# A planned instruction order for a recurrent attention kernel: weight loads with release times, one shared DMA server in the planner, and a priority for each tile and row

## The chip, the cores and the metric

The kernel runs on one core of a Trainium2 chip. Five instruction streams work side by side: TensorE (PE; its weight loads are shown apart as PEld), VectorE (DVE), ScalarE (ACT), GpSimd (POOL) and SyncE (SP), which here only issues DMAs. Each stream takes its instructions strictly in the order in which they were written, and waits at an instruction until what it needs is there. The metric is the device time of one execution in microseconds; lower is better. The kernel before takes 223.28 us (median of 3 executions, 223.24 to 225.57). The profiled execution shows a span of 219.2 us from the first to the last instruction; the span leaves out 4.1 us that the metric counts.

## The reference, cut to what matters

The inputs r, k, v, w, a and b are [batch 4, heads 8, time 768, 40] in 32-bit floats. A 40x40 state for each batch and head goes through the 768 steps:

```
y[t]  = r[t] @ state
Sa    = state @ a[t]
state = state * w[t] - outer(Sa, b[t]) + outer(v[t], k[t])
```

The heads of y are put side by side to x, [4, 768, 320], and a mixing layer follows:

```
theta = x @ w_theta                     # 320x320
y     = w_tok_r @ (x*cos(theta)) + w_tok_i @ (x*sin(theta))   # both 768x768, over time
u     = x + y
out   = u + relu(u @ w_ch)              # 320x320
```

The token matrices mix all 768 steps of a batch, so no output row of a batch can be finished before all of its x is known.

## The kernel before, in words

**Tiles.** Time is cut into chunks of 128 steps, six to a batch, so there are 24 tiles (batch x chunk), numbered 0 to 23. All eight heads of a tile are worked on together. For each tile there are six loads of 160 KB (w, k, b, a, r, v; `loads`, L398, issued by SP) into buffers that exist four times (`raw_w`, `raw_kb`, `raw_a`, `raw_rv`). The innermost run of a load is one head's 40 floats, 160 bytes.

**Work of a tile.** `prep`: ACT takes the logarithm of w (`ln`, L407), PE sums it over time (`cs`, L414 to L424), ACT takes the exponential (`exp`, L429), POOL scales k, b and a with it and casts r and v (`kb`, `ah`, `rv`, L436 to L445; for tiles 0 and 1 DVE and ACT do this), PE transposes the results (`tkb`, `ta`, `trv`, L380) and ACT copies the transposes out of PSUM. `scores`: 64-row matmuls (L468) and a masking by DVE (L473), four times a tile. `recurrence`: `x0`, `nu`, `gt`, `gd`, `nut`, which pass the state from one tile of a batch to the next. `readout`: y, and x from it (`y`, `ex`, `xt`). `theta` (`th`, L616): three 320-column matmuls by `wth`, copied to a buffer. Once a half batch has its thetas, ACT computes cosines and sines (`sines`), which needs another ACT table than `ln` and `exp`, and POOL multiplies them with x (`z`, L652).

**Rows of the mixer.** `mix_row`, six to a batch, 24 in all: 12 matmuls of 320 columns (L671) against the transposed token matrices, an add (`uadd`, DVE), a transpose (`ut`), the product by `wch` (`ch`, L616), the last step on DVE (`oo`, L691) and the store by SP (`st`, L695). Row j needs block j of both token matrices.

**Weights.** POOL issues all weight loads: `wth` and `wch` in two DMAs each (`mixer_weights`, L701 and L704), and for each of six blocks of 128 rows one DMA for either token matrix (`wtok_block`, L712) into staging buffers `wrow`, two for each matrix. PE transposes a block (`wt`, L720) and DVE copies it into place, which sets the staging buffer free for the block after the next.

**Who sets the order.** The kernel writes its own order. Every step above is an `Op` with an engine, a modelled cost, what it reads and writes, and a priority; `Plan.order` runs a simulation in which, whenever an engine is free, the ready operation with the least `priority + wait * (time it would idle)` is taken. The instructions are then emitted in the order of planned start. Nothing of the plan's times exists on the chip: there only the order on each engine is left, and the semaphores. In the kernel before, the priority is `PERIOD * tile + OFF[kind]` (and `ROWLAG`, `ROWSTEP` for rows), so all tiles follow one rhythm; SP's and POOL's DMAs have two servers with separate queues in the plan; PE changing between 64-row and 128-row matmuls costs 91 ns in it. The six loads of tiles 0, 1 and 2 and those of tile 3 are ready at once, and so are the loads of `wth`, `wch` and of the first two token blocks.

Of the kernel before, what the change touches and what calls it, by code (L numbers as in the profile page):

```python
# [17 lines left out]
LAT = {("PE", "ACT"): 36, ("PE", "DVE"): 38, ("ACT", "PE"): 52, ("DVE", "PE"): 52,  # L18
       ("POOL", "PE"): 53, ("ACT", "DVE"): 33, ("ACT", "POOL"): 77}
OVERLAP = {"ACT": 94, "DVE": 83, "POOL": 50}  # L20
FREE0 = {"PE": 800, "ACT": 2100, "DVE": 4400, "POOL": 3600, "SP": 740}
BANKS = 8
DOUBLE = 4


class Op:
    __slots__ = ("eng", "kind", "i", "fn", "cost", "tail", "reads", "writes", "prio",
                 "mode", "table", "new", "spare", "pre", "nsucc", "start", "end", "idx",
                 "npre", "succ", "work", "banks", "soft", "loose")


class Plan:
# [7 lines left out]
    def add(self, eng, kind, i, fn, cost, reads=(), writes=(), prio=0.0, mode=128,  # L40
            tail=0, table=None, new=None, spare=0, work=0, after=(), loose=False):
        o = Op()
        o.eng, o.kind, o.i, o.fn, o.cost, o.prio = eng, kind, i, fn, cost, prio
        o.mode, o.tail, o.table, o.new, o.spare, o.work = mode, tail, table, new, spare, work
        o.reads, o.writes, o.loose = reads, writes, loose
        o.idx = len(self.ops)
# [18 lines left out]
    def order(self, wait=47.7, tswitch=11847.0):  # L65
        ops = self.ops
        for o in ops:
            o.succ = []
            o.npre = len(o.pre)
            o.start = o.end = None  # L70
            o.banks = None
        users = {}
        for o in ops:
            for k in set(o.reads) | set(o.writes):
                if k[0] == "ps":
                    users.setdefault(k, set()).add(o)
# [7 lines left out]
        for o in ops:  # L84
            for p in o.pre:
                p.succ.append(o)
            for p in o.soft:
                p.succ.append(o)
        left = {k: len(v) for k, v in users.items()}
# [8 lines left out]
        dma = [0.0, 0.0]  # L98
# [9 lines left out]
        def make_ready(o):  # L108
            t = 0.0
# [21 lines left out]
        while len(out) < n:  # L131
            pick = None
            for e, lst in ready.items():
                if not lst:
                    continue
                te = free[e]
                cand = []
                lo = None
                for o in lst:
# [8 lines left out]
                    if e == "PE" and o.mode != mode:  # L148
                        t += 91
# [6 lines left out]
                for t, o, b in cand:  # L156
                    s = o.prio + wait * (t - lo)
                    if e == "ACT" and o.table is not None and o.table != table:
                        s += tswitch
# [21 lines left out]
            elif o.work:  # L181
                q = 0 if o.eng == "SP" else 1
                iss = 430 if o.eng == "SP" else 890
                free[o.eng] = t + iss
                s = max(dma[q], t + iss + 900)
                if q == 1 and dma[0] > s:
                    dma[0] += o.work
                    dma[1] = s + 2 * o.work
                else:
                    dma[q] = s + o.work  # L190
                o.end = dma[q] + 1000
# [26 lines left out]
def tail(n):  # L218
# [3 lines left out]
OFF = dict(load=-32.72, ln=-14.21, cs=-14.27, exp=-12.91, kb=-24.2, ah=-17.45, rv=-8.81,  # L222
           tkb=-12.03, ekb=-12.49, ta=-6.68, ea=-13.73, spsi=-4.74, mpsi=3.81, sphi=-3.67,
           mphi=-0.3, trv=-7.1, erv=-4.13, slv=-1.2, mlv=12.94, x0=-1.29, nx=-1.28,
           nu=-1.19, enu=-4.96, gt=3.22, egt=5.53, gd=-0.91, egd=-4.34, nut=0.71,
           enut=-1.87, slu=0.59, mlu=4.85, y=4.31, ex=0.1, xt=7.27, ext=6.43, th=11.06,
           eth=17.93, sin=5.35, z=1.67, row=13.39, uadd=1.12, ut=13.16, eut=16.3, ch=19.9,
           oo=11.33, st=19.28, wdma=-32.85, wt=-13.25, ewt=-5.52)
PERIOD = 7.54
ROWLAG = 7.44  # L230
ROWSTEP = 7.6
# [3 lines left out]
def kernel(  # L235
# [130 lines left out]
    def prio(kind, i):  # L366
        return 1000.0 * (PERIOD * i + OFF[kind])

    def add(eng, kind, i, fn, cost, reads=(), writes=(), pr=None, **kw):
        return plan.add(eng, kind, i, fn, cost, tuple(reads), tuple(writes),  # L370
                        prio(kind, i) if pr is None else pr, **kw)
# [16 lines left out]
    def evac(eng, kind, i, psk, dst, n, reads=(), writes=()):  # L388
        if eng == "ACT":
            add(eng, kind, i, lambda: copy_words(dst, ps(psk)[:, 0:n // 2]),  # L390
                190 + n / 2.4, [psk], writes)
# [409 lines left out]
```

## Time and profile before

| What | Value |
|---|---|
| Time (median of 3) | 223.28 us |
| Span of the profiled execution | 219.2 us |
| PE busy | 198.0 us, 90% |
| DVE busy | 167.2 us, 76% |
| ACT busy | 147.1 us, 67% |
| POOL busy | 119.2 us, 54% |
| Bytes moved by DMA | 30.81 MB, mean 141 GB/s |
| A load of one of the six inputs, issue to landing | 3.7 to 4.1 us (medians) |
| A load of a token block, issue to landing | 4.7 and 5.1 us (medians) |

Busy times of an engine count the time in which at least one of its instructions is under way. Matmuls overlap: one of 320 columns lasts some 300 ns in the trace, while the next starts 136 ns later. So a PE that is shown busy all the time may still be waiting between short bursts, and how densely it works is better read from the spacing of its starts. Besides the busy times, the profile gives the busy share in 40 slices of the span, the chain of work that ended last, waits by who waited for whom, and tables by stage.

### The profile page before, as it was taken

How to read it: one execution, taken by the hardware profiler on the slowest of the kernel's cores; microseconds unless marked ns; L12 is line 12 of the kernel's file. 1: busy time of each engine (PE TensorE's matmuls, PEld its weight loads, DVE VectorE, ACT ScalarE, POOL GpSimd, SP SyncE). 2: the span in 40 equal slices, each digit the busy share in tenths (PEclk: the TensorE clock that was granted, in tenths of full speed). 3: DMA queues.
4: the chain of work that ended last, by engine and by line, in shares of the span. 5: the costliest groups of instructions: out<-in, count | busy, mean ns of one | idle time of the engine just before them, and what ended most of it. 6: DMA issues, size and time to landing. Idle time of an engine off the chain costs nothing.

```text
span 219.2 us, 8154 instructions
## 1 busy us (share of the span) xinstructions
PE 198.0 (90%) x3368; PEld 155.4 (71%) x3368; DVE 167.2 (76%) x250; ACT 147.1 (67%) x319; POOL 119.2 (54%) x184
## 2 busy tenths in 40 slices
PE   1519999889987999999999999999999999999992
PEld 1418778667776788878778778877877788776671
DVE  7336899885898759898598878869888889975532
ACT  3316755886769984996689766987698759563110
POOL 5600536798737791794938644986187507514000
PEclk9999999999999999999999999999999999999999
DMA  6999999999999899999999999999980000100121
GB/s 113 199 185 191 154 168 174 176 178 152 174 187 170 152 172 185 153 155 189 191 187 155 178 189 183 167 184 190 178 182 33 3 33 30 34 33 30 64 88 60
DMA packets 155684, 30.81 MB, mean 141 GB/s; under 512 B 150400, under 2 KB 155648, under 8 KB 155648
## 3 DMA queue, kind: packets, MB, share of 16 engines
q1 hardware_dynamic: 153216, 27.54, 68.9%
q0 software_dynamic: 2432, 2.77, 8.0%
q8 instruction: 26, 0.43, 0.8%
q14 instruction: 10, 0.08, 0.1%
HBM read 29.13 MB, written 3.93 MB: 151 GB/s over the span
## 4 chain that ended last, share of the span: by engine, by line
PE 74%; DMA 7%; DVE 6%; POOL 3%; ACT 3%; issue 3%; SPq 2%; DVEq 0%; ACTq 0%; POOLq 0%
PE ps_s L671 18%; PE ps_s L380 15%; PE ps_d L468 11%; PE ps_s L616 9%; DMA raw_w<-in_w_dram 7%; PE ps_s L572 4%; PE ps_s L538 2%; PE ps_s L520 2%; SPq L398 2%; PE ps_s L602 2%; PE ps_s L508 2%; DVE lamu L473 2%; PE ps_s L600 2%; DVE psi L473 2%; PE ps_s L502 1%
## 5 line engine op out<-in xcount | busy, mean ns | idle before, releaser
L436 POOL TENSOR_TENSOR kb<-raw_kb,ex 128x320 bf16<-128x320 f32 x44 | 37.1, 863 | 49.7 <-ACT ex L429 49.1
L671 PE MATMUL ps_s<-zr,wtok_r 128*128 128x320 bf16 x144 | 40.8, 300 | 0.0
L671 PE MATMUL ps_s<-zi,wtok_i 128*128 128x320 bf16 x144 | 40.7, 299 | 0.0
L473 DVE TENSOR_TENSOR lamu<-ps_d,mask_p 128x1024 bf16<-128x1024 f32 x24 | 29.3, 1221 | 5.3 <-PE ps_d L468 4.6
L473 DVE TENSOR_TENSOR psi<-ps_d,mask_p 128x1024 bf16<-128x1024 f32 x24 | 29.2, 1216 | 5.3 <-PE ps_d L468 5.3
L473 DVE TENSOR_TENSOR lamv<-ps_d,mask_p 128x1024 bf16<-128x1024 f32 x24 | 29.2, 1218 | 5.0 <-PE ps_d L468 2.7
L473 DVE TENSOR_TENSOR phi<-ps_d,mask_n 128x1024 bf16<-128x1024 f32 x24 | 29.3, 1219 | 1.9 <-PE ps_d L468 1.6
L445 POOL CAST rv<-raw_rv 128x320 bf16<-128x320 f32 x44 | 19.1, 452 | 16.0 <-DMA raw_rv<-in_r_dram 8.8
L652 POOL TENSOR_TENSOR zr<-cs,x 128x320 bf16<-128x320 f32 x23 | 17.9, 792 | 10.3 <-ACT cs L640 10.2
L383 ACT COPY rvT<-ps_s 128x512 f32<-128x512 f32 x24 | 14.2, 590 | 9.2 <-PE ps_s L380 9.0
L383 ACT COPY uT<-ps_s 128x192 f32<-128x192 f32 x24 | 7.7, 320 | 17.4 <-PE ps_s L572 13.9
L429 ACT ACTIVATE ex<-ps_d 128x656 f32<-128x656 f32 x24 | 17.2, 718 | 2.9 <-PE ps_d L424 2.0
L383 ACT COPY kbT<-ps_s 128x512 f32<-128x512 f32 x24 | 14.0, 584 | 7.5 <-PE ps_s L380 7.1
L440 POOL TENSOR_TENSOR ah<-raw_a,ex 128x320 bf16<-128x320 f32 x22 | 19.0, 866 | 0.0
L468 PE MATMUL ps_d<-aT,kbT 64*128 64x128 bf16 x384 | 18.3, 223 | 0.7 <-ACT aT L383 0.5
L380 PE MATMUL ps_s<-ident,kb 128*128 128x128 bf16 x192 | 15.9, 227 | 2.5 <-DVE kb L436 1.3
L652 POOL TENSOR_TENSOR zi<-cs,x 128x320 bf16<-128x320 f32 x23 | 17.9, 793 | 0.0
L681 DVE TENSOR_TENSOR u<-ps_s,x 128x320 bf16<-128x320 f32 x24 | 11.8, 490 | 8.0 <-PE ps_s L671 7.5
L671 PEld LDWEIGHTS <-wtok_r 128*128 128x128 bf16 x144 | 14.0, 98 | 4.5
L671 PEld LDWEIGHTS <-wtok_i 128*128 128x128 bf16 x144 | 14.1, 98 | 3.8
L407 ACT ACTIVATE lw<-raw_w 128x320 bf16<-128x320 f32 x24 | 11.2, 478 | 7.6 <-DMA raw_w<-in_w_dram 7.4
L691 DVE SCALAR_TENSOR_TENSOR oo<-ps_s,u 128x320 f32<-128x320 f32 x24 | 11.7, 488 | 5.8 <-PE ps_s L616 5.1
(109 smaller groups left out, 552.6 us busy)
## 6 DMA issues: line engine op xcount, KB each, us to landing
raw_w<-in_w_dram SPq DMA_DIRECT2D x24, 160.0 KB, 4.0
raw_kb<-in_k_dram SPq DMA_DIRECT2D x24, 160.0 KB, 4.1
raw_kb<-in_b_dram SPq DMA_DIRECT2D x24, 160.0 KB, 3.9
raw_a<-in_a_dram SPq DMA_DIRECT2D x24, 160.0 KB, 4.0
raw_rv<-in_r_dram SPq DMA_DIRECT2D x24, 160.0 KB, 3.9
raw_rv<-in_v_dram SPq DMA_DIRECT2D x24, 160.0 KB, 3.7
out_dram<-oo SPq DMA_DIRECT2D x24, 160.0 KB, 1.9
wrow_r<-in_moe_w_tok_r_dram POOLq DMA_DIRECT2D x6, 192.0 KB, 4.7
```

What stands on the lines that cost most here:

```text
L380: nc.tensor.transpose(out=dst[:, c:c + 128], in_=pair(src, g), identity=ident)
L383: nc.scalar.copy(out=out.bitcast(FP32), in_=in_)
L429: add("ACT", "exp", i, lambda: nc.scalar.activation(out=ex, in_=ps(pk)[:, :, 0:328], func=AF.Exp), 740, [pk], [kex], table="lnexp")
L436: lambda j=j: (nc.vector if fast else nc.gpsimd).tensor_tensor(out=kb[:, j, :, 0:D], in0=raw_kb[s4][:, j], in1=invW, op=ALU.mult),
L440: lambda: (nc.vector if fast else nc.gpsimd).tensor_tensor(out=ah[:, :, 0:D], in0=raw_a[s4], in1=Wi, op=ALU.mult),
L445: lambda j=j: (nc.scalar.copy if fast else nc.gpsimd.tensor_copy)(out=rv[:, j, :, 0:D], in_=raw_rv[s4][:, j]),
L468: nc.tensor.matmul(t[:, q, g, :], lhsT=lhs[rows(q), g * 128:(g + 1) * 128], rhs=rhs[rows(q), g * 128:(g + 1) * 128], start=True, stop=True)
L473: add("DVE", kindm, i, lambda: nc.vector.tensor_tensor(out=dst.rearrange("p a b c -> p (a b) c"), in0=ps(p).rearrange("p a (g c) -> p (a g ...
L616: nc.tensor.matmul(dst, lhsT=lhs[:, kt, :], rhs=rhs[:, kt, :], start=kt == 0, stop=kt == 2)
L652: nc.vector if fast else nc.gpsimd).tensor_tensor(
L671: nc.tensor.matmul(ps(pk)[:, 0:DM], lhsT=wtok[nm][:, s, j * 128:(j + 1) * 128], rhs=zs[c][:, s], start=n == 0 and c == 0, stop=n == NT - 1 ...
L681: add("DVE", "uadd", q, lambda: nc.vector.tensor_tensor(out=u[:, 0:DM], in0=ps(pk)[:, 0:DM], in1=x[:, 0:DM], op=ALU.add), 480, [pk, ("x", ...
```

## The change

The computation, the tiles, the buffers and the instructions are the same; what changes is the planner's picture of the chip and the priorities, and with them the order on every engine.

- **Weight loads.** Each weight load gets a release time (`rel`, eight numbers in units of 1000 ns): before it, the plan does not regard the load as ready. `wth` is released at once, `wch` at 28.5, and the blocks of the token matrices 0 to 5 at 59.76, 33.74, 24.97, 97.39, 29.98 and 104.9. The purpose is that the loads of the first tiles have the DMA engines to themselves.
- **One DMA server.** SP's and POOL's DMAs now share one server in the plan; SP is taken as blocked when more than 3600 ns of transfers are outstanding, and the modelled cost of an input load rises from 910 to 1030 ns, of a token block from 1100 to 1240.
- **Priorities.** `PERIOD * tile` and the row rhythm are replaced by one number for each of the 24 tiles and each of the 24 rows (`TIMES`), with new offsets for each kind of step (`OFF`). They need not rise from tile to tile.
- **Weights of the rule.** `wait` goes from 47.7 to 416.01 and the penalty for an ACT table switch from 11847 to 546374.
- **Costs.** The cost of changing into 64-row matmuls is 95 ns and out of them 120 ns; several operations' costs are set anew by 3 to 15%.

```diff
-    def order(self, wait=47.7, tswitch=11847.0):
+    def link(self):
...
+            o.prio = 1000.0 * (TIMES[o.spec[0]][o.spec[1]] + OFF[o.spec[2]])
...
         def make_ready(o):
-            t = 0.0
+            t = 0.0 if o.release is None else 1000.0 * TIMES["rel"][o.release]
...
                 te = free[e]
+                if e == "SP":
+                    te = max(te, dma - SP_DEPTH)
...
                     if e == "PE" and o.mode != mode:
-                        t += 91
+                        t = max(t, te + (INTO64 if o.mode == 64 else OUTOF64))
...
-                    s = o.prio + wait * (t - lo)
+                    s = o.prio + WAIT * (t - lo)
                     if e == "ACT" and o.table is not None and o.table != table:
-                        s += tswitch
+                        s += TSWITCH
...
-                q = 0 if o.eng == "SP" else 1
-                iss = 430 if o.eng == "SP" else 890
-                free[o.eng] = t + iss
-                s = max(dma[q], t + iss + 900)
-                if q == 1 and dma[0] > s:
-                    dma[0] += o.work
-                    dma[1] = s + 2 * o.work
-                else:
-                    dma[q] = s + o.work
-                o.end = dma[q] + 1000
+                free[o.eng] = t + o.cost
+                if o.eng == "SP":
+                    dma = max(dma, t + 1350.0) + o.work
+                    o.end = dma + 600.0
+                else:
+                    s = max(t + 1800.0, dma - SP_DEPTH)
+                    dma = max(dma, s) + o.work
+                    o.end = min(dma, s + 2.0 * o.work) + 1000.0
...
-PERIOD = 7.54
-ROWLAG = 7.44
-ROWSTEP = 7.6
...
+WAIT, TSWITCH = 416.01, 546374.0
+TIMES = dict(
+    tile=[
+        -39.53, -34.24, -29.51, -3.78, 20.04, 41.89, 38.94, 51.03, 56.49, 58.19, 71.7, 90.01,
+        94.38, 97.37, 114.43, 121.89, 126.37, 125.37, 126.65, 137.15, 152.75, 154.06, 155.36,
+        173.39],
...
+    rel=[
+        -29.38, 28.51, 59.76, 33.74, 24.97, 97.39, 29.98, 104.9])
...
-            add("POOL", "wdma", 0, go, 890, [], [(key, 0)], work=500, pr=-500.0 if key == "wth" else 1e4)
-            add("POOL", "wdma", 0, go2, 890, [], [(key, 1)], work=130, pr=-500.0 if key == "wth" else 1e4)
+            n = 0 if key == "wth" else 1
+            add("POOL", "wdma", n, go, 580, [], [(key, 0)], at="rel", work=1030, release=n)
+            add("POOL", "wdma", n, go2, 580, [], [(key, 1)], at="rel", work=260, release=n)
...
-            add("POOL", "wdma", i, lambda row=row, ap=ap: nc.gpsimd.dma_start(
-                out=row, in_=ap[tb * 128:(tb + 1) * 128, :]), 890, [],
-                [("wrow", nm, tb % 2)], work=1100)
+            add("POOL", "wdma", 2 + tb, lambda row=row, ap=ap: nc.gpsimd.dma_start(
+                out=row, in_=ap[tb * 128:(tb + 1) * 128, :]), 580, [],
+                [("wrow", nm, tb % 2)], at="rel", work=1240, release=2 + tb)
```

The built programs show the order that comes out, engine by engine; the steps of the prediction name the places of it that they use.

## The prediction

> **What bounds the kernel now.** I read the page's slices first.
>
> ```profile
> span 219.2 us, 8154 instructions
> PE 198.0 (90%) x3368; PEld 155.4 (71%) x3368; DVE 167.2 (76%) x250; ACT 147.1 (67%) x319; POOL 119.2 (54%) x184
> ...
> PE   1519999889987999999999999999999999999992
> ...
> DMA  6999999999999899999999999999980000100121
> ...
> q1 hardware_dynamic: 153216, 27.54, 68.9%
> q0 software_dynamic: 2432, 2.77, 8.0%
> ```
>
> Two resources are full, at different times. The DMA engines are full from 5 us to 165 us (30 slices of 9), then almost idle. PE has holes in the first 14 slices and none afterwards. The table by stage says how large the holes are:
>
> ```profile
> core 0: us, PE busy (x) PEld busy (x) DVE busy (x) ACT busy (x) POOL busy (x), PEclk, DMA share, GB/s
> 0.00:16.00 16.00, 4.49 (x44) 3.39 (x45) 7.72 (x47) 4.75 (x9) 6.78 (x20) 1.00 1.01 167
> 16.00:80.00 64.00, 58.28 (x1093) 47.16 (x1092) 50.45 (x61) 48.21 (x105) 40.54 (x61) 1.00 1.03 172
> 80.00:201.50 121.50, 121.40 (x2131) 95.59 (x2126) 101.89 (x127) 91.37 (x199) 71.86 (x104) 1.00 0.70 132
> 201.50:219.20 17.70, 13.80 (x107) 9.26 (x107) 7.11 (x15) 2.77 (x8) 0.00 (x0) 1.00 0.19 66
> ```
>
> PE idles 11.5 us before 16 us, 5.7 us up to 80 us, 0.1 us up to 201.5 us (the start of tile 23's `th`), and 3.9 us in the tail. What ended the first hole stands in ScalarE's timeline, and what lay ahead of the late load in GpSimd's:
>
> ```profile
> 3.69 0.47 ACT L407 ACTIVATE lw<-raw_w 128x320 bf16<-128x320 f32 x1 [1.67 <-DMA raw_w<-in_w_dram]
> 15.50 0.47 ACT L407 ACTIVATE lw<-raw_w 128x320 bf16<-128x320 f32 x1 [4.61 <-DMA raw_w<-in_w_dram]
> ...
> 6.84 0.57 POOL L712 DMA_DIRECT2D wrow_r<-in_moe_w_tok_r_dram  x1
> 7.38 0.57 POOL L712 DMA_DIRECT2D wrow_i<-in_moe_w_tok_i_dram  x1
> 7.90 0.58 POOL L712 DMA_DIRECT2D wrow_r<-in_moe_w_tok_r_dram  x1
> 8.42 0.59 POOL L712 DMA_DIRECT2D wrow_i<-in_moe_w_tok_i_dram  x1
> ```
>
> The chain of work that ended last has the same waits in it:
>
> ```profile
> 6.03 9.44 DMA raw_w<-in_w_dram
> ...
> 56.56 7.00 DMA raw_w<-in_w_dram
> ```
>
> Tile 1's w is issued at 6.03 us and lands at 15.5 us, where a load of w takes 4.0 us in the median: eight weight DMAs (four of `wth` and `wch`, four of token blocks) are in front of or beside it. Tile 8's w has the same fate at 56.56 us, beside two token-block loads issued at 55.7 and 56.3 us.
>
> **How dense PE is.** Busy time flatters PE, so I counted its work from the starts in the trace: 56 ns from one transpose to the next, 136 ns for 320 columns, 25 ns for 40, 35 ns for 80; going from transposes into 64-row matmuls takes 151 ns (95 beyond the 56), coming out 148 (122 beyond 26). Multiplied by the program's instructions, the whole is 185.1 us. Up to the `th` of tile 7 the count is 53.8 us, and the trace starts it at 80.5: lag 26.7. Up to tile 23's `th` it is 172.0, start 201.5: lag 29.5. So in 121 us PE loses only 2.8; of the lag, nine tenths arises before 80 us, while DMA is the limit. That is the stretch in which the change can earn.
>
> **What the skill says.** The Trainium skill, "DMA: Bandwidth & Descriptors", section Issuing engines are not separate DMA queues: DMAs from SP and from GpSimd run on the same 16 engines and interleave. The trace agrees (9.44 against 4.0 us). So the single server is the right picture, and postponing weights moves no work away, it only reorders it. "Perfetto Trace Analysis", section Tensor Engine Instruction: the end of a matmul in a trace is an estimate; hence the count by starts. "TensorEngine Tiling (Array Packing)", section Key Properties: changing the tiling mode drains PE; here 95 + 122 = 217 ns a pair.
>
> **The change, part by part.**
>
> *Weights.* At the start the new order issues only `wth`; `wch` comes after tile 3's operands on GpSimd, then blocks 1, 0, 2, 4, 3, 5 in that order, each after the operands of a later tile. I need the price of a load. Between the landing of tile 0's w (3.6 us) and tile 8's w (63.6 us) lie 48 input loads and 15.0 us of weights: q0 takes 8.0% of 219.2 us, 17.5 us, for all weights, by size 1.24 for each of the twelve token loads, of which ten fall in here, and 2.6 for `wth` and `wch`. That leaves (60 - 15)/48 = 0.935 us a load, 5.6 a tile. In the new order tile 1's w lands at 3.6 + 5.6 + 1.3 = 10.5 us (before 15.5), tile 4's at 27.3, tile 7's at 47.9, tile 8's at 53.5 (before 63.6), tile 9's after block 0 at 61.6, tile 10's after block 2 at 69.8, tile 11's after block 4 at 77.9 (before, its logarithm starts at 82.9). Blocks 3 and 5 follow at tiles 13 and 14, which by then are not what PE waits for. The DMA total stays, and its end near 165 us has 36 us in hand.
>
> *What PE makes of it.* Counted in the new order, the work before a tile's `cs` is 37.7 us (tile 8), 44.7 (9), 51.9 (10), 59.3 (11), 67.4 (12). A tile's `cs` can start some 0.6 us after its w lands, which gives lags of 16.4, 17.5, 18.5, 19.2 and 16.7. The largest, 19.2, is the floor that DMA sets. In the kernel before, the floor was tile 8's (64.8 - 40.3 = 24.5) and 2.2 us came on top until tile 7's `th`, as PE had run dry and filled again through exponential, scaling and transposes. I put the same 2.2 on top: 21.4, against 26.7. This is 5.3 us less.
>
> *Mode changes.* 136 changes become 124: six pairs of 217 ns, 1.3 us of PE work, all in the dense stretch. Four row matmuls more and the weight of two changes lie after tile 23's `th` instead of before, so the count up to it is 169.5, 2.5 less.
>
> *Tail.* The count from that `th` to the last row's last matmul is 12.6 against 12.1 us, and at the end two rows finish together (two adds on VectorE, transposes, two `ch`), where before only one did: I take 0.3 more, by the 0.49 us of an add partly hidden. Tail 18.5 instead of 17.7.
>
> *Order of the tiles.* Tile 6 goes ahead of 5 and 17 ahead of 16, by the batches' independence. It costs nothing if loads keep the same order, and they do on SP. New rates for `exp`, `nx` and so on change no instruction. ACT table loads remain 14, 1.28 us each.
>
> *New waits.* GpSimd's block loads now stand between operand steps. A block whose staging buffer is still being transposed would hold the operands behind it, and PE would wait for those; before, the longest such wait was 1.6 us. I take 0 (PE's transposes of the earlier block stand well ahead), up to 3 us. Two stores are now issued back to back, behind which loads wait on SP; SP's four-deep buffers hide this, 0 to 1 us.
>
> Sum: lag up to tile 23's `th` 21.4 + 2.8 = 24.2, so it starts at 169.5 + 24.2 = 193.7; with the tail 212.2, 7.0 us under 219.2. The time is then 223.3 - 7.0 = 216.3 us.
>
> **The rivals.**
>
> *DMA-tight (20%).* The 2.2 us on top vanish, since the new order has rows or other work between a late `cs` and what follows it: 214 us. For it speaks that before tile 9's transposes 4 us of other work is queued; against it, that no rows can start before token blocks are there.
>
> *Given back (15%).* The postponed blocks hit tiles 9 to 14 and the rows, which are the filler for PE, start later (first row after 49.6 us of counted work, before after some 48): then the lead of 5 us at the start is lost by 100 us as the total of DMA up to there is the same, and only the mode changes remain, 223.3 - 1.3 + 0.8, about 222.8.
>
> *Ill-fitting order (10%): slower.* With `wait` nine times as high, the new order is packed by planned times; if the DMA arrives otherwise than planned, engines that take instructions in order hold each other up. The old order loses 2.8 us in 16 tiles, 0.17 a tile; at 0.8 a tile it would be 13 us, 10 more, and 216.3 + 10 = 226. Against it: the new costs (load 1030 ns, `exp` 717, 95 and 120 for changes) are near the trace's durations (0.935 us, 718 ns, 95, 122), and loads come earlier than planned, not later.
>
> **How the numbers follow.** The main case has 55%. Faster by over 1% (under 221.0): nearly all of it and DMA-tight, 0.78. Within 1%: most of "given back" and a bit of the main case, 0.11. Slower: the ill-fitting order and an upper end of new waits, 0.11. The range goes from 212.5 (DMA-tight less the whole of 1.5 us of in-stretch loss) to 222.5 (GpSimd waits of 3 us and half of "given back").
>
> **What would show it.** Tile 1's `ln` near 10.5 us, tile 8's near 54; idle PE before 80 us down from 17.2 us to about 12; DMA full until about 165 us as before; the `th` of tile 23 near 194 us; the tail 18 to 19 us. I am wrong if GpSimd waits at a token-block load, if PE gets holes after 80 us, or if tile 1's w lands as late as before.

## The result and the profile after

The changed kernel takes 220.53 us (median of 5 executions, 219.36 to 220.73), against 223.28 (222.03 to 225.57, 5 executions) on the same chip: ratio 0.990, 95% interval 0.985 to 0.995. That is 2.75 us less, where the prediction said 7.0. A short dip of the granted clock costs some 1.1 us (the changed kernel's spans are 217.5 us at clock 1.0 and 218.5 to 218.8 at 0.992). In each execution with both numbers the span is 1.8 to 1.9 us shorter than the time; the 4.1 us named ahead of the prediction set the span of one execution against the median of others. The traced execution of the kernel before thus took about 221.1 us (an estimate, 219.2 + 1.9), less than any of the five that were timed.

The page of the changed kernel, in the same lines as before, with the clock:

```profile
span 217.5 us, 8118 instructions
PE 197.0 (91%) x3368; PEld 155.8 (72%) x3368; DVE 166.0 (76%) x250; ACT 146.9 (68%) x319; POOL 118.4 (54%) x184
...
PE   1487898888898899999999999999999999999993
...
PEclk9999999999999999999999999999999999999999
DMA  6998989989998999999978999899897010101022
...
q1 hardware_dynamic: 153216, 27.54, 70.3%
q0 software_dynamic: 2432, 2.77, 7.8%
```

PE starts earlier (slice 3 is 8 instead of 1), but then stands mostly at 8 up to slice 14, where the kernel before mostly had 9. Its table by stage (each engine's busy time, with the number of instructions in brackets):

```profile
core 0: us, PE busy (x) PEld busy (x) DVE busy (x) ACT busy (x) POOL busy (x), PEclk, DMA share, GB/s
0.00:16.00 16.00, 8.04 (x98) 6.15 (x99) 9.54 (x50) 7.05 (x13) 3.39 (x14) 1.00 1.01 161
16.00:80.00 64.00, 55.27 (x1061) 43.90 (x1060) 49.77 (x58) 47.03 (x103) 41.25 (x63) 1.00 0.99 167
80.00:201.50 121.50, 121.20 (x2113) 97.06 (x2112) 100.20 (x129) 90.64 (x198) 73.75 (x108) 1.00 0.73 135
201.50:217.50 16.00, 12.51 (x102) 8.70 (x100) 6.49 (x14) 2.13 (x7) 0.00 (x0) 1.00 0.21 73
```

PE's idle time ahead of 16 us fell from 11.5 to 8.0 us; from 16 to 80 us it rose from 5.7 to 8.7. Together 16.7 instead of 17.2: the hole moved and did not close. ScalarE's timeline shows that the load did come earlier (the logarithms of tiles 1 and 8, `lw`, and what stands ahead of the first):

```profile
11.84 0.43 ACT L530 CAST nx<-ps_s 128x320 bf16<-128x320 f32 x1 [1.43 <-PE ps_s L524]
12.16 0.47 ACT L423 ACTIVATE lw<-raw_w 128x320 bf16<-128x320 f32 x1
...
60.15 0.47 ACT L423 ACTIVATE lw<-raw_w 128x320 bf16<-128x320 f32 x1
```

In the kernel before both lines ended in a bracket that named a DMA; tile 1's is in the prediction, tile 8's is this:

```profile
63.58 0.47 ACT L407 ACTIVATE lw<-raw_w 128x320 bf16<-128x320 f32 x1 [0.53 <-DMA raw_w<-in_w_dram]
```

Now no bracket stands there: the logarithms of tiles 1 and 8 wait for no load. Their w had landed at 10.5 and 55.9 us. Tile 1's logarithm stands behind tile 0's `nx`, which waits for PE.

How PE's time divides can be said more sharply with the prediction's count by starts ("count" is the TensorE work that the program has in a stretch, counted so; a start less the count ahead of it is its lag). Up to the first matmul of the first row, and from there to the end:

| | tile 1's `cs` | tile 0's `th` | tile 7's `th` | first row | count up to it | end | row to end | count |
|---|---|---|---|---|---|---|---|---|
| before | 16.0 | 25.0 | 80.5 | 73.6 | 47.1 | 219.2 | 145.6 | 137.9 |
| after | 12.8 | 20.5 | 76.0 | 76.4 | 50.0 | 217.5 | 141.1 | 133.6 |

Up to the first row PE has 2.9 us more work and takes 2.8 us longer; after it, 4.3 us less work and 4.5 us less time. So of the 1.7 us of span 1.4 is TensorE work that is not there any more (185.0 against 183.6 us, nearly all of it mode changes; no run changed these alone); of the 5.3 us of idle time that the held-back loads were to save, nothing is left at the first row.

### The profile page after: what moved, and what is told of

It is laid out like the page before. It is cut to its first block, busy times and chain, and to the rows that moved or that the text cites. A ratio compares the mean times of both kernels' runs of the same rounds, so it can differ in the third digit from the quotient of the medians.

```text
span 217.5 us, 8118 instructions
## 1 busy us (share of the span) xinstructions
PE 197.0 (91%) x3368; PEld 155.8 (72%) x3368; DVE 166.0 (76%) x250; ACT 146.9 (68%) x319; POOL 118.4 (54%) x184
## 3 DMA queue, kind: packets, MB, share of 16 engines
q1 hardware_dynamic: 153216, 27.54, 70.3%
## 4 chain that ended last, share of the span: by engine, by line
PE 71%; DVE 10%; DMA 7%; POOL 4%; issue 4%; ACT 2%; SPq 1%; POOLq 0%; DVEq 0%; ACTq 0%
PE ps_s L685 19%; PE ps_s L396 14%; PE ps_d L484 9%; PE ps_s L631 8%; DMA raw_a<-in_a_dram 4%; PE ps_s L588 4%; DVE lamu L489 3%; DMA wrow_i<-in_moe_w_tok_i_dram 3%; PE ps_s L617 2%; DVE phi L489 2%; PE ps_s L536 2%; POOL kb L452 2%; DVE psi L489 2%; PE ps_s L554 2%; PE ps_s L524 2%
## 5 line engine op out<-in xcount | busy, mean ns | idle before, releaser
L452 POOL TENSOR_TENSOR kb<-raw_kb,ex 128x320 bf16<-128x320 f32 x44 | 37.4, 862 | 18.1 <-ACT ex L445 12.5
L489 DVE TENSOR_TENSOR lamv<-ps_d,mask_p 128x1024 bf16<-128x1024 f32 x24 | 29.1, 1219 | 6.2 <-PE ps_d L484 6.1
L489 DVE TENSOR_TENSOR phi<-ps_d,mask_n 128x1024 bf16<-128x1024 f32 x24 | 29.1, 1217 | 0.8 <-PE ps_d L484 0.7
L445 ACT ACTIVATE ex<-ps_d 128x656 f32<-128x656 f32 x24 | 17.2, 719 | 7.4 <-PE ps_d L440 6.4
L461 POOL CAST rv<-raw_rv 128x320 bf16<-128x320 f32 x44 | 18.6, 451 | 0.0
L484 PE MATMUL ps_d<-aT,kbT 64*128 64x128 bf16 x384 | 16.8, 221 | 1.5 <-ACT ex L445 0.7
L695 DVE TENSOR_TENSOR u<-ps_s,x 128x320 bf16<-128x320 f32 x24 | 11.7, 488 | 8.1 <-PE ps_s L685 7.9
L624 DVE TENSOR_TENSOR x<-ps_s,ex 128x320 bf16<-128x320 f32 x24 | 11.7, 487 | 6.3 <-PE ps_s L617 5.5
L617 PE MATMUL ps_s<-kb,lamu 128*128 128x40 bf16 x192 | 15.0, 180 | 1.3 <-DVE lamu L489 1.2
```

The lines of the kernel that those rows point to most:

```text
L445: add("ACT", "exp", i, lambda: nc.scalar.activation(out=ex, in_=ps(pk)[:, :, 0:328], func=AF.Exp), 717, [pk], [kex], table="lnexp")
L452: lambda j=j: (nc.vector if fast else nc.gpsimd).tensor_tensor(out=kb[:, j, :, 0:D], in0=raw_kb[s4][:, j], in1=invW, op=ALU.mult),
L461: lambda j=j: (nc.scalar.copy if fast else nc.gpsimd.tensor_copy)(out=rv[:, j, :, 0:D], in_=raw_rv[s4][:, j]),
L484: nc.tensor.matmul(t[:, q, g, :], lhsT=lhs[rows(q), g * 128:(g + 1) * 128], rhs=rhs[rows(q), g * 128:(g + 1) * 128], start=True, stop=True)
L489: add("DVE", kindm, i, lambda: nc.vector.tensor_tensor(out=dst.rearrange("p a b c -> p (a b) c"), in0=ps(p).rearrange("p a (g c) -> p (a g ...
L617: nc.tensor.matmul(o, lhsT=lamu[:, p, g, :], rhs=kb[:, 1, h, 0:D], start=False, stop=True, skip_group_check=True)
```

## Theories and experiments

**Theory "order":** once tile 1 has its w, no load limits the first 76 us; a tile's own chain (sum, exponential, scaling, transposes, masks, recurrence) over four engines in a fixed order does. **Rival "loads":** DMA still sets the floor, by loads other than those of w. **Rival "one engine":** VectorE's masks, ScalarE's sines or copies, or GpSimd took DMA's place. **Rival "nothing gained":** the early loads are worth nothing in either order. Times of marks come from the traces; ratios are against the kernel before on the same chip (other chips than that of the result).

### Weight loads early again, in the new order

```diff
+    shift(lambda o: o.kind == "wdma" and o.i in (1, 3), lambda o: o.kind == "wdma" and o.i == 0)
+    shift(lambda o: o.kind == "wdma" and o.i == 2, lambda o: o.kind == "wdma" and o.i == 0)
```

(`shift` moves operations within the finished order; here `wch` and token blocks 0 and 1 go behind `wth`.)

> The changed kernel with its order kept on every engine, except that GpSimd issues w_ch and token blocks 1 and 0 at the start, as the kernel before did. Theory 'order': PE's lag up to about 76 us is set by the order in which sums, operands and rows stand, and the loads had 3 to 8 us in hand; then the lead of tile 1 is lost, but the th of tile 7 stays within 1.5 us of the 76.0 us of the changed kernel, and the time is 220 to 222 us. Theory 'DMA pace' (mine): the loads set the lag; tiles 1 to 4 come 5 us later, tile 7's th comes at 79 to 81 us and the time is 223.5 to 226 us.

Measured: 223.59 us, ratio 0.993 (0.990 to 0.996). ScalarE's timeline:

```profile
3.60 0.47 ACT L423 ACTIVATE lw<-raw_w 128x320 bf16<-128x320 f32 x1 [1.59 <-DMA raw_w<-in_w_dram]
15.72 0.47 ACT L423 ACTIVATE lw<-raw_w 128x320 bf16<-128x320 f32 x1 [2.16 <-DMA raw_w<-in_w_dram]
```

Tile 1's w is late again, by 5.2 us, and the delay is handed on stiffly: tile 0's `th` at 25.0 (after: 20.5), tile 3's 51.6 (46.6), tile 7's 82.0 (76.0, one of the 6.0 us being a clock dip), although by tile 8 the loads have caught up (w at 57.2 against 55.9). From the first row to the end it takes 141.1 us, like the changed kernel. At full clock its spans are some 3 to 5 us longer. So in the new order the start is worth its full length, and of the loads moved here only tile 1's counts: "nothing gained" falls for this order. Tile 7's `th` (81 us without the dip) and the time lie where "DMA pace" had put them, not "order"; what "DMA pace" says of the later tiles is tested by the half loads below.

The run shows one thing more. Tile 0's `th` is as late as in the kernel before (25.0 in both), and 4.2 us less counted work stands ahead of tile 7's; yet that comes no earlier (81 against 80.5). The new order itself loses up to there about what the early loads win.

### The hold alone, with the old priorities

```diff
-            t = 0.0
+            t = o.release
...
-                 work=500, pr=-500.0 if key == "wth" else 1e4)
+                 work=500, pr=-500.0 if key == "wth" else 1e4,
+                 release=0.0 if key == "wth" else 28510.0)
```

> The kernel before with one addition to its planner: release times for w_ch (28.5) and token blocks 0 and 1 (28.5 and 33.7), all else as before, so that w_ch and the two blocks are issued behind the operands of tiles 3 to 5. Theory 'order': holding back alone brings tile 1 forward by 5 us, and the time moves by less than 1.5 us, 222 to 224.5. Theory 'DMA pace': it brings what was forecast without the mode changes and the tail, 217 to 219.5 us.

Measured: 225.83 us, ratio 1.003 (1.000 to 1.007): no gain, and above the range of either theory. The plan is made anew with these release times, so the order on the engines differs too (TensorE's from its 220th matmul on). Its executions ran at a lower clock (0.959 to 0.985) than those of the kernel before beside it (0.98 to 1.0), so its trace says little on where the time went; in it tile 1's sum was at 12.4 us and tile 7's `th` at 86.1, so the early start was lost before the first row.

### Loads of half the size, and token blocks of 8 rows

```diff
-            add("SP", "load", i, lambda dst=dst, src=src: nc.sync.dma_start(out=dst, in_=src),
+            add("SP", "load", i, lambda dst=dst, src=src: nc.sync.dma_start(
+                out=dst[:, 0:4], in_=src[:, 0:4]),
```

> The changed kernel in its order, with each of the 144 input loads fetching 4 of 8 heads only (the other heads are constants set once), so that the output is not the reference's; the DMA time of an input load halves. Theory 'DMA pace': the th of tile 7 comes 10 us or more earlier than 76 us and the time falls to 205 to 211 us. Theory 'order': loads land far ahead, but the chains of sum, exponential, operands, masks and recurrence and what stands between them hold PE all the same; th of tile 7 comes 0 to 5 us earlier and the time is 215 to 221 us.

```diff
-                out=row, in_=ap[tb * 128:(tb + 1) * 128, :]), 580, [],
+                out=row[0:8, :], in_=ap[tb * 128:tb * 128 + 8, :]), 580, [],
```

> The changed kernel in its order, with every token-block load fetching 8 of 128 rows (the rest of the staging buffer is zero, so the token matrices and the output are not the reference's); all waits stay, the DMA time of the blocks goes. Theory 'DMA pace': 5 to 7 us of DMA time ahead of tile 11 vanish and the time falls by 3 to 6 us, to 214.5 to 217.5 us. Theory 'order': by under 2 us, 218.5 to 220.5 us; what is gained is the wait of PE for the transposes of block 2 near 74 us.

Measured: 217.43 us (0.966; 0.961 to 0.971) and 218.67 us (0.971; 0.965 to 0.977). With half loads the DMA engines have a third of their time free in the stretch (the last number but one, 0.66):

```profile
0.00:16.00 16.00, 9.34 (x113) 7.10 (x113) 11.09 (x53) 8.12 (x18) 7.24 (x30) 1.00 0.79 125
16.00:80.00 64.00, 55.47 (x1075) 44.37 (x1076) 49.71 (x58) 47.03 (x103) 43.08 (x65) 1.00 0.66 104
```

PE is busy 55.47 us of 64, in the changed kernel 55.27. All that is won is won at tile 1: its sum starts at 11.1 instead of 12.8, tile 7's `th` is at 74.0 instead of 76.0, the end at 215.5 instead of 217.5; with the tiny blocks 11.8, 74.7 and 216.2. From tile 1's sum to the end it is 204.7 us in the changed kernel, 204.4 with half loads, 204.4 with tiny blocks. "Loads" falls for the new order: with half of every load taken away, all that follows tile 1's sum gets 0.3 us shorter. Both runs lie in the ranges of "order", though what the tiny blocks win is the start, and not the wait for block 2 that was expected.

### The changed kernel again, and three suspects

```diff
+
```

> The changed kernel as it is, beside the kernel before and the following runs on one chip. Nothing is told apart by it; it gives the base: 219.4 to 221 us, tile 7's th at 76 us of the span, 0.985 to 0.995 of the kernel before.

```diff
+    order = [o for o in order if not (o.kind == "sin" and o.i < NCH)]
```

> The changed kernel in its order, without the four cosine and sine instructions of the first batch and the four table loads around them (a constant takes their place, so the output is not the reference's). Theory 'ScalarE': two loads and two functions in one go, about 4.5 us each time, hold the next tile's exponential and copies, and PE with them, at 40 and at 68 us; without them tile 7's th comes 4 to 7 us earlier than 76 and the time falls by as much. Theory 'VectorE': masks and recurrence set the pace of 7.9 us a tile; tile 7's th comes under 2 us earlier, and only the first row, which waits for the products with the cosines, comes earlier.

```diff
-            out=dst.rearrange("p a b c -> p (a b) c"), ...
+            out=dst[:, 0], in0=ps(p)[:, 0].rearrange("p (g c) -> p g c", c=128), ...   # i < 8
```

> The changed kernel in its order; for tiles 0 to 7 each of the four masks covers half of the columns (0.7 instead of 1.2 us; the rest is zero, so the output is not the reference's), which takes 2 us a tile off VectorE. Theory 'VectorE': the pace of 7.9 us a tile falls to 6 to 7 and tile 7's th comes 7 to 12 us earlier. Theory 'ScalarE': the masks' latency alone gives 1 to 4 us.

```diff
-    wrow = dict(r=sb("wrow_r", [128, S], BF16, 2), i=sb("wrow_i", [128, S], BF16, 2))
+    wrow = dict(r=sb("wrow_r", [128, S], BF16, 3), i=sb("wrow_i", [128, S], BF16, 3))
...
+    shift(lambda o: o.kind == "wdma" and o.i == 4, lambda o: o.kind == "wdma" and o.i == 2)
```

> The changed kernel with a third pair of staging buffers, and the loads of block 2 right behind those of block 0 on GpSimd, so that GpSimd no longer waits 3.0 us for PE's transposes and PE no longer for block 2 at 74 us; all other orders kept. If these waits are on the path, the first row comes 1.5 to 3 us earlier than 76.4 and the time falls by 1 to 3 us; if rows wait for the products with the sines anyway, it stays within 0.7 us.

| | time | ratio (interval) | tile 1's `cs` | tile 7's `th` | end |
|---|---|---|---|---|---|
| again | 220.0 | 0.979 (0.974 to 0.985) | 12.0 | 75.1 | 216.6 |
| no sines, first batch | 217.96 | 0.973 (0.970 to 0.977) | 11.7 | 74.6 | 216.1 |
| half masks, tiles 0 to 7 | 217.32 | 0.969 (0.964 to 0.974) | 11.2 | 73.5 | 215.2 |
| third staging buffer | 219.9 | 0.984 (0.979 to 0.989) | 12.7 | 75.5 | 217.1 |

The changed kernel, run again, ends 204.6 us after tile 1's sum: its scatter is that of the first loads. The third buffer shows how a wait can mislead. GpSimd's timeline of the changed kernel has the wait that the prediction feared:

```profile
68.69 0.59 POOL L725 DMA_DIRECT2D wrow_r<-in_moe_w_tok_r_dram  x1 [3.00 <-PE ps_s L733]
69.27 0.54 POOL L725 DMA_DIRECT2D wrow_i<-in_moe_w_tok_i_dram  x1
```

and in the chain that ended last, that load stands right ahead of the first row, with a load of `a` further up:

```profile
43.12 3.70 DMA raw_a<-in_a_dram
...
69.27 5.63 DMA wrow_i<-in_moe_w_tok_i_dram
76.52 1.36 PE ps_s L685 x10
```

With a third buffer the block is issued 8 us earlier:

```profile
60.72 0.55 POOL L725 DMA_DIRECT2D wrow_r<-in_moe_w_tok_r_dram  x1
61.24 0.56 POOL L725 DMA_DIRECT2D wrow_i<-in_moe_w_tok_i_dram  x1
```

and the end is still 204.4 us after tile 1's sum. A second path of about the same length must run beside it. The same holds for the `a` load, which half loads took away. By the ends, the sines give 0.5 us against the run again and half masks 1.4, but of this 0.3 and 0.8 are tile 1's earlier sum, and a clock dip lengthens the half masks. Cleaner is the way from tile 1's sum to tile 5's `th`, which in the new order comes after tile 6's, right ahead of tile 7's, and before any of these dips: 51.2 us in the changed kernel and in the run again, 50.8 without sines, 49.2 with half masks. A mask takes 1.22 us, half a mask 0.69, and the chain names 17 masks before 64 us; were they the only path, half masks would give some 9 us, and they give 2.0.

### Several made lighter together

```diff
+ (half loads, half masks and no sines, as above, in one kernel)
```

> The changed kernel in its order with three things lightened at once: input loads of 4 of 8 heads, half-width masks for tiles 0 to 7, no sines in the first batch (constants in their place; the output is not the reference's). If one of the three hid behind another, the sum gives more than the parts: tile 7's th falls from 75 to 62 to 68 us. If a chain of short dependences across all engines, in a fixed order, sets the pace, the parts add at most: 70 to 73 us, and the time is 213 to 217 us.

```diff
+            m = n // 2 if 4 <= i < 8 else n
+            add(eng, kind, i, lambda: copy_words(dst[:, 0:m], ps(psk)[:, 0:m // 2]),
...
+        hs = slice(0, 4 if 4 <= i < 8 else 8)   # heads that kb, ah and rv work on
```

> On top of the kernel with half loads, half-width masks in tiles 0 to 7 and no sines for the first batch, for tiles 4 to 7 only half the heads are scaled and cast by GpSimd and only half of each transposed operand is copied by ScalarE; that part of the output is not computed. From tile 3's to tile 7's theta product the counted TensorE work is 22.9 us in all of these kernels; the changed kernel takes 29.4 us, the kernel with three parts lighter 28.9, of which about 1.2 was a short dip of the clock, so 27.7. Theory (a tile's own chain runs over all engines, and what is left of the idle time is the sum of many short waits on each): the waits on ScalarE and GpSimd, 2.8 of the 6 us, shrink by about half, so 26.0 to 26.8 us from tile 3 to tile 7, and the whole kernel 1 to 2 us under the one with three parts lighter at the same clock. Rival (what is left is TensorE's own: its work is undercounted or its written order makes it wait on itself): 27.5 to 28 us, no gain.

The same edit on the changed kernel alone:

> The changed kernel with only this lighter: for tiles 4 to 7 GpSimd scales and casts half the heads and ScalarE copies half of each transposed operand; the other half is left out of the computation. Theory (a chain over all engines, none of which is the bound): from tile 3's to tile 7's theta product 28.0 to 28.8 us instead of 29.3, as the waits on VectorE's masks (3.2 us) stay or grow; the whole 0.5 to 1.3 us less. Rival (ScalarE or GpSimd is the bound of the stretch): up to 3 us less, 26.5 us from tile 3 to tile 7. Rival (TensorE's own work is what fills the stretch): no change, 29.2 to 29.5.

| | time | ratio (interval) | tile 3's `th` | tile 7's `th` | between | less the dip | end |
|---|---|---|---|---|---|---|---|
| after | 220.53 | 0.990 (0.985 to 0.995) | 46.6 | 76.0 | 29.4 | 29.4 | 217.5 |
| three lighter | 214.66 | 0.955 (0.947 to 0.963) | 42.3 | 71.2 | 28.9 | 27.7 | 212.7 |
| all lighter | 213.17 | 0.955 (0.949 to 0.960) | 41.6 | 69.7 | 28.1 | 26.9 | 211.2 |
| copies and scalings | 219.35 | 0.982 (0.976 to 0.988) | 46.4 | 76.7 | 30.3 | 29.1 | 218.2 |

The dip is seen in the clock's slices of the one with all lighter:

```profile
PE   1798889999988999999999999999999999999993
...
PEclk9999999999996999999999999999999999999999
```

By the ends, three lighter give 3.9 us against the run again, where half loads, sines and half masks alone give 1.1, 0.5 and 1.4. From tile 1's sum to tile 5's `th`, ahead of the dips, it is:

| changed, again | half loads | no sines | half masks | these three | all lighter | copies and scalings alone |
|---|---|---|---|---|---|---|
| 51.2 | 51.2 | 50.8 | 49.2 | 47.7 | 46.3 | 51.0 |

Together the three give 3.5 us, their parts alone 0.0, 0.4 and 2.0: more than the sum, as when several paths have nearly the same length and what one lets go another holds. It is far from the 62 to 68 us for tile 7's `th` that one hidden limit would have brought (71.2, within the 70 to 73 of the other theory).

Lightening ScalarE's copies and GpSimd's scalings on top gives 0.8 us between the tiles' `th` and 1.5 at the end: a little less between them than the theory's 0.9 to 1.7, but not the rival's nothing. Alone, that edit gives next to nothing without the dip (29.1 against 29.2 to 29.4), which misses the theory's 28.0 to 28.8 and is what the rival "TensorE's own work" expected. The tally of PE's starts says why it gives so little: between the two `th`, PE loses 6.6 us to others in the changed kernel (3.2 to VectorE, 1.6 to ScalarE, 1.5 to GpSimd, some nowhere), and with lighter copies and scalings 4.1 to VectorE, 1.3 and 0.4. What GpSimd gives up VectorE takes. That speaks for a set of paths of nearly one length, with VectorE's masks the largest part, and for no one engine. Counted work there is 22.9 us, so even with all lighter 4 us of 26.9 stay; whether latencies or the written order hold those was not separated.

### The old order with a light start, and two more traces of it

```diff
+                if dst is wch:
+                    nc.gpsimd.dma_start(out=dst[0:8, 0, :], in_=src[0:8, :])
...
-                out=row, in_=ap[tb * 128:(tb + 1) * 128, :]), 890, [],
+                out=row[0:(8 if tb < 2 else 128), :],
+                in_=ap[tb * 128:tb * 128 + (8 if tb < 2 else 128), :]), 890, [],
```

> The kernel before in its own order, with w_ch and token blocks 0 and 1 fetched in 8 rows each (the rest is zero, so the output is not the reference's): the loads ahead of tiles 1 to 5 lose about 6 us of DMA time and nothing is moved. It is the most that holding back could bring in the old order. Theory 'rigid order': tile 1's sum starts at 11 instead of 16 us, the old order waits for nothing else in its place, tile 7's th comes at 75 to 77 instead of 80.5 us, and the time falls by 3 to 5 us to 218.5 to 220.5. Theory 'refilled wait' (the tile's own chain takes the place of the load): tile 7's th comes under 2 us earlier and the time is 221.5 to 223.5 us.

> The kernel before once more, for a second trace of it; nothing is changed. Its first trace (span 219.2 us) is 1.7 us longer than that of the changed kernel, while the medians of time differ by 2.75, and on another chip by 4.1. Theory A (the first trace is a lucky execution: the loads that its order waits for, at tiles 1, 6 and 8 and again at tiles 14 to 17, come at other moments in each execution): span 221 to 223, tile 1's sum still at 16.0, and the surplus in waits for loads, so that the lag at the first row or between tiles 13 and 18 is 2 to 4 us larger. Theory B (the clock): span 219 to 220 at full clock, and more only by 1.1 us for each short dip.

> The kernel before a third time, for a third trace; nothing is changed. As for the second: theory A expects a span of 221 to 223 us with the surplus in waits for loads, in other places than in the second trace; theory B expects 219 to 220 us at full clock.

(The last two change nothing.)

| old order | time | tile 1's w lands | its `cs` | tile 7's `th` | tile 15's `th` | tile 23's `th` | end |
|---|---|---|---|---|---|---|---|
| first trace | 223.28 (median) | 15.5 | 16.0 | 80.5 | 141.7 | 201.5 | 219.2 |
| second | 221.67 | 12.5 | 13.0 | 79.7 | 141.8 | 202.1 | 219.8 |
| third | 221.45 | 11.6 | 12.2 | 80.7 | 141.8 | 201.8 | 219.6 |
| light start | 219.78 (median; the traced one 220.94) | 8.9 | 10.4 | 76.5 | 140.8 | 201.4 | 219.1 |

This was the surprise of the study. The same kernel, on other executions, gets tile 1's w 3 to 4 us earlier by chance, and ends no earlier. With `wch` and two blocks almost taken away, tile 1 leads the first trace by 5.6 us, and tiles 7 to 12 by 4.0; then the lead goes, to 2.4 at tile 14, 0.9 at tile 15 and 0.1 at tile 17. Both numbers that "rigid order" expected did come (tile 7's `th` at 76.5, the time 219.78), and by time the light start gains: ratio 0.979 (0.971 to 0.987), where the kernel before had a median of 225.84. The spans of the traces don't show that gain (219.1 against 219.2 to 219.8). In the traces about half of the lead ends at one place. GpSimd's timeline in the light start:

```profile
131.00 0.45 POOL L449 CAST rv<-raw_rv 128x320 bf16<-128x320 f32 x1 [4.40 <-DMA raw_rv<-in_r_dram]
```

and in the first trace of before:

```profile
131.33 0.45 POOL L445 CAST rv<-raw_rv 128x320 bf16<-128x320 f32 x1 [1.62 <-DMA raw_rv<-in_r_dram]
135.95 0.45 POOL L445 CAST rv<-raw_rv 128x320 bf16<-128x320 f32 x1 [1.70 <-DMA raw_rv<-in_r_dram]
```

The cast of tile 18's r starts at 131.0 to 132.4 us in all four traces, whatever came before: whoever is early waits longer (4.40 against 1.62). Behind it in GpSimd's queue stands tile 17's `kb`, and PE waits for that (1.3 us in the light start, 0.1 in the first trace). From 80 to 170 us PE loses 4.7 us in the light start and 1.0 in the first trace; of this 2.1 and 0.1 go to `kb`, most of the rest to VectorE. GpSimd waits there 13.5 us for loads of r in the light start, 8.8 in the first trace of before, and in the changed kernel for none of r, and 4.0 us for v. By the traces, then, the old order has a second floor near tile 17, in good part by loads, that swallows an early start, and the new order shows none. No run took these loads away, and the gain by time stands against it: that an early start is worthless in the old order is not shown.

Of the two theories on the traces, neither fits whole: the spans (219.8 and 219.6) are those of theory B, the loads that move are those of A. The three traced executions of the kernel before took some 221.1, 221.67 and 221.45 us, and the shortest of some 60 others on record 221.74 (in one series the spans are 221.1 to 223.0 at almost the same clock). Why the traced ones are the shorter stays open.

### The planner's numbers

```diff
-        -39.53, -34.24, -29.51, -3.78, 20.04, 41.89, 38.94, 51.03, ...
+        -39.53, -34.24, -29.51, -3.78, 20.04, 38.94, 41.89, 51.03, ...
```

> The changed kernel planned anew with the priorities of tiles 5 and 6 exchanged, so that the first batch is loaded and finished before the next one begins. If tile 6 ahead of 5 delays the rows, and rows are what fills PE, the first row comes 3 us earlier or more and the time falls by 2 us or more, to 217 to 219. If the fit of all priorities to each other counts for more, the time rises, to 221 to 226 us, with more waits of PE.

```diff
-                650, [], [key], work=1030)
+                650, [], [key], work=935)
```

> The changed kernel planned anew with 935 instead of 1030 ns for an input load, the price that I had worked out from the kernel before. If the order is late because the plan has loads land late, sums start 2 to 4 us earlier at tiles 2 to 9 and the time falls by 1 to 4 us. If the priorities fit only the price they were set for, it rises to 221 to 226 us.

Measured: 223.96 us, ratio 1.000 (0.995 to 1.005), and 229.05 us, ratio 1.018 (1.008 to 1.028). Both reach tile 7's `th` at 75.6 and 74.9, like the changed kernel, and lose later: from the first row to the end 145.7 us instead of 141.1, 1.8 of it more counted work, in the first; and in the second a first row at 85.3 with a tail of 23 us. The first lies where its expectation put "the fit counts for more", the second even above that range: with the load's price as worked out from the trace the planner makes an order that is 4 us worse than the kernel before. So the priorities fit one set of modelled prices, and this one truer price did not make a better order.

## Why the prediction was wrong, point by point

**The step that failed** is "A tile's `cs` can start some 0.6 us after its w lands", from which came "the floor that DMA sets", 19.2, and with 2.2 on top the lag 21.4. The landings were near: 10.5 for tile 1 as forecast, 28.9 (27.3), 50.7 (47.9), 55.9 (53.5), 62.1 (61.6), 70.3 (69.8), 78.1 (77.9) for tiles 4, 7, 8, 9, 10, 11. But the sums start at 12.8, 32.2, 55.0, 60.9, 68.6, 78.3 and 85.7: 2.3 to 8.0 us after the landing. Tile 7's `th` is at 76.0, where the count is 49.6: lag 26.4, as in the kernel before (26.7). That is 5.0 us over the forecast, and all but 0.3 of the span's error (217.5 against 212.2).

What the runs show in its place: in the new order loads set the pace only at the start, and then the order itself, with its chains over all engines. Half loads leave 55.2 of the 55.5 us from tile 0's `th` to tile 7's. The 0.6 us were no invention: in the first trace of before, the sums of tiles 0, 1, 6 and 8 start 0.5 to 1.2 us after their w. I carried this over to an order in which it holds for tile 0 alone, and took DMA engines that are full where PE has holes for the cause of the holes. The pace could not have told: before, the stretch takes 7.9 us a tile, and loads with the weights among them 7.5 (60 us for eight tiles, by the prediction's own working; 5.6 is a tile's loads without weights). In the changed kernel the landings of w come every 6.6 us, and the `th` still every 7.9.

The second thing left out is what the new order costs by itself. From tile 0's `th` to tile 3's it takes 26.2 us, and 26.2 with half loads, where the old order takes 22.2 to 22.5 in all four traces; the counted work differs by 1.4. So the lead in time falls from 4.5 us at tile 0's `th` to 4.0, 1.8 and 0.6 at those of tiles 1 to 3. At tile 7's it is 4.5 again only because 4.2 us of work was moved behind that (six pieces of token-block transposes come before it, where ten and a row did); by lag the lead goes 3.4, 2.0, 1.4, 0.9, and 0.3 at tile 7. Which step of the order costs this was not separated.

**Mode changes, 1.3 us:** the count of the whole fell 1.4, and this is most of the 1.7 us by which the first traces differ. The Trainium skill, "TensorEngine Tiling (Array Packing)", section Key Properties, says that a change of mode drains PE; the trace of the changed kernel agrees, with 152 ns from a transpose into 64-row matmuls and 148 out of them, as before.

**Growth from tile 7 to tile 23:** 3.4 us for 2.8. **Tail:** 18.2 for 18.5. **DMA:** the last input load lands at 167.6 us (before 164.3), for "near 165"; right.

**New waits on GpSimd, taken as 0:** one of 3.0 us came, at block 2's load, and cost nothing (the third buffer).

**"I am wrong if":** none of the three signs decided it. GpSimd did wait at a token-block load, without effect; tile 1's w was early, and PE had no new holes after 80 us. What showed the error were the marks beside them: the logarithms of tiles 1 and 8 at 12.2 and 60.2 us, not near 10.5 and 54, and idle PE before 80 us of 16.7 us, not "about 12".

**The rivals:** "given back" came nearest (222.8 us for 220.53; mostly the mode changes remain) with a wrong place: the lead went mostly between tiles 0 and 3, not through the postponed blocks up to 100 us, and the tiny blocks and the third buffer show that these blocks do not hold the rows. "DMA-tight" shares the failed step. "Ill-fitting order" did not happen here, but it did in the plan with the load at 935.

**From span to time:** 2.75 us in the medians is more than the 1.7 in the first traces; the changed kernel's traces lie at 216.6 and 217.5, those of before at 219.2 to 219.8, so 1.7 to 3.2. On a second chip the medians differ by 4.1. What is above the 1.4 us of counted work is not explained.

**Slips in the working:** faster by over 1% got 0.78, but the two cases named for it have 0.75 together. Of the 30 DMA slices called 9, 27 are 9, two 8 and one 6. The count ahead of the first row is 50.0 against 47.1, not 49.6 against "some 48". None of these makes the error.

## What to carry to other kernels

A full DMA queue beside a starved engine is no proof that loads set the pace, and neither is a like pace of both (7.9 and 7.5 us a tile here). Look whether instructions behind a load really wait for it at most tiles, in the order that will run and not only in the old one, and in a second trace; and take half of the loads away, which here told it at once. A new order has a price of its own: run it with the old start, as "weights early" did, before adding up what its parts should bring. In a written order a lead is handed on until a place that waits for something not moved by it; look for that place (here, by the traces, near 131 us in the old order) before counting the lead as gain. And a long piece in the chain that ended last is worth its length only if no other path is as long, which a kernel without that piece tells.

## What was not expected of the hardware

- The same first loads, issued in the same order, land at different times from one execution to the next: tile 1's w in the kernel before at 11.6, 12.5 and 15.5 us. The Trainium skill, "DMA: Bandwidth & Descriptors", section Issuing engines are not separate DMA queues, says that DMAs of SP and GpSimd interleave on the same engines; the traces agree (up to 9.4 us from issue to landing, where 4.0 is the median), and show that the landings are not repeated. With only `wth` in front, tile 1's w varies less: 9.8 to 10.5 us in four traces (changed, again, third buffer, copies and scalings).
- The dips of the granted clock are stretches of 3.4 us at half of the full clock (one of the ten in these traces lasts 10.2 us). Such a dip costs about 1.1 us: from tile 5's to tile 7's `th` of the new order it is 12.8 to 13.1 us with one and 11.7 to 12.1 without. They come in kernels with full and with lightened loads; ahead of nine of the ten PE had been busy for only 0.9 to 1.9 us of the 3.4 us just before, ahead of the tenth for 2.6. If such a hole is the cause, which no run tested, an edit that opens one pays for it twice.
